# GeGLU feed-forward on one core: the first loads reordered and split by halves of D, the first products regrouped

## The chip, the core and the metric

The kernel runs on one core of a Trainium2 chip. The metric is the device time of one execution in microseconds (us), taken as the median of repeated runs. Beside the timed runs there is one execution that was profiled; all rows below come from it.

## What is computed

```python
B, S, D, F = 32, 32, 1024, 3584        # bf16: x [B, S, D], w_gate and w_up [D, F], w_down [F, D]

def reference(x, w_gate, w_up, w_down):
    return (_gelu(x @ w_gate) * (x @ w_up)) @ w_down      # _gelu: the tanh form
```

There are 1024 tokens (B times S). F is cut into 28 blocks of 128 columns, D into 8 slices of 128.

## The kernel before

**Stage 1** forms `gT`, the gated activations with F on the partitions. It does not multiply the gate and the up product separately. For one block `i` of 128 columns of F it treats the pair (gate, up) and the pair (first 512 tokens, second 512 tokens), with D cut into two halves, as one 2 by 2 block product, and computes it with seven half-size products instead of eight (Strassen's scheme in Winograd's form). A product is four matmuls, one for each 128-row slice of a half of D, each with 512 tokens moving.

The names of the seven products follow the code. The tokens' side: `xt0` holds the first 512 tokens transposed, with halves of D `B11` and `B21`; `xt1` holds the second 512 with `B12` and `B22`. VectorE (DVE) makes from them `T1 = B12 - B11`, `T2 = B22 - T1`, `T3 = B22 - B12`, `T4 = B21 - T2` (line 157, ten instructions, in this order) and ScalarE (ACT) copies `B22`. The weights' side: `a11`, `a12` are the two halves of D of a block of w_gate, `a21`, `a22` those of w_up. For each block the sums `S1 = a21 + a22` (line 166), `S3 = a11 - a21` (line 167), `S2 = S1 - a11` (line 171) and `S4 = a12 - S2` (line 175) are made. `early_sums` makes S1 and S3, `second_sum` S2, `late_sums` S4. S2 is always made by DVE; the others by DVE for the first blocks, and by GpSimd (POOL) later.

- `first_product` (P1) and `second_product` (P2) are the gate of the first tokens: they need only `xt0` and w_gate, and both end in PSUM tile `a`. ACT copies `a` after P1 to SBUF (tile `e1`, line 187) and applies the gelu after P2 (line 193).
- `seed` puts the copy back into another PSUM tile, `X`, on which P6 (S2 with T2), P7 (S3 with T3) and P4 (C22, a copy of a22, with T4) add up in turn. Between them ACT copies `X` out: `E2` after P6 (line 214) and `e3` after P7 (line 227). P4 may only start on `X` when the copy `e3` is done.
- P5 (S1 with T1) and P3 (S4 with B22) add up in PSUM tile `Y`. DVE adds `Y` and `e3` to `U1` (line 229) before P3, and `Y` and `E2` to `h1` (line 234) after it; ACT applies the gelu to `h1` (line 236); `finish` (line 239) multiplies.

PSUM has eight banks here: four for `X` (tag p) and four that `A` and `Y` use in turn (tag q).

Nothing is scheduled by a planner: the order of each engine's instructions is the order in which the code is written (`tc.manual_schedule()`), and tiles add the waits. At the start, 18 matmuls on a zeroed tile (line 137) run while the first loads are under way. All loads go through the queue of SyncE (SP) in program order, except the first half of w_gate tile 0, which ACT issues after the fourth of those matmuls. A w_gate tile (`load_gate`, line 84) holds two blocks of F, 0.52 MB; `load_up(0, 0, 2)` (line 91) brings w_up for blocks 0 and 1, also 0.52 MB; each transposing load of 512 tokens is 1.05 MB.

Since T1 to T4 need the second tokens, the kernel first does P1 of blocks 0 to 7 and P2 of blocks 0 to 6 ("ahead", `LEAD = 8`): 60 matmuls. Then come P5 of blocks 0 and 1 (line 271), P1 of 8 and P2 of 7, P6 of 0 and of 1, P7 of 0 and of 1, P1 of 9 and P2 of 8, P4 of both, P3 of both. The loop over the blocks 2 to 27 follows; it keeps P1 and P2 two blocks ahead through `ahead()`. In it POOL's tiles S1, S3 and S4 have two buffers each, so block `i` reuses those of block `i - 2`.

After `T4`, POOL copies eight elements of it to a tile `held` (line 252). The copy's value is not used: it makes POOL wait until DVE has made T4.

**Stage 2** multiplies `gT` by w_down with the same seven-product scheme (lines 328 to 485) and stores the result.

Of the kernel before, what the change touches and what calls it, by code (L numbers as in the profile page):

```python
# [7 lines left out]
ACT = mybir.ActivationFunctionType  # L8
# [4 lines left out]
def kernel(  # L13
# [35 lines left out]
    assert N == 2 * NB and DT % 2 == 0 and D % DB == 0 and FT % 4 == 0  # L49
    NWARM = 18  # L50
    LEAD = 8
# [29 lines left out]
    def load_gate(c, queue, lo=0, hi=DT):  # L81
        if c not in WG:
            WG[c] = gw.tile([P, DT, 2 * P], bf16, name="gw", tag="gw")
        queue.dma_start(
            out=WG[c][:, lo:hi, :], in_=wg_r[:, lo:hi, 2 * c * P : (2 * c + 2) * P]
        )
# [41 lines left out]
    with tc.manual_schedule():  # L128
# [5 lines left out]

        nc.sync.dma_start_transpose(out=xt0, in_=xf[0:NB, :])
        for n in range(NWARM):
            nc.tensor.matmul(warm[n % 4], lhsT=zt[:, 0:P], rhs=zt, start=True, stop=True)
            if n == 3:
                nc.scalar.activation(table, warm[n][:, 0:8], ACT.Copy)
                load_gate(0, nc.scalar, 0, KH)  # L140
        load_gate(0, nc.sync, KH, DT)
        load_gate(1, nc.sync)
        load_up(0, 0, 2)
        load_gate(2, nc.sync)
        load_gate(3, nc.sync)
        nc.sync.dma_start_transpose(out=xt1, in_=xf[NB:N, :])
        load_gate(4, nc.sync)
# [33 lines left out]

        def first_product(i):
            A[i] = psum_q("a")
            product(A[i], a11(i), B11)
            if i % 2 == 0:
                E1[i // 2] = ring.tile([P, 2, NB], fp32, name="e1", tag="ring")
            nc.scalar.activation(E1[i // 2][:, i % 2, :], A[i], ACT.Copy)  # L187

        def second_product(i):
            product(A[i], a12(i), B21, first=False)  # L190
            if i % 2 == 0:
                GL[i // 2] = half.tile([P, 2, NB], bf16, name="gl0", tag="half")
            nc.scalar.activation(GL[i // 2][:, i % 2, :], A[i], ACT.Gelu_apprx_tanh)

# [5 lines left out]

        done = 0

        def ahead():
            nonlocal done
            if done < FT:
                first_product(done)
            if done:
                second_product(done - 1)
            done += 1

        def sixth_product(i):
            product(X[i], S2[i], T["T2"], first=False)
            E2[i] = epool.tile([P, NB], fp32, name="e2", tag="e2")
            nc.scalar.activation(E2[i], X[i], ACT.Copy)  # L214

# [7 lines left out]

        def seventh_product(i):
            product(X[i], S3[i], T["T3"], first=False)
            e3 = epool.tile([P, NB], fp32, name="e3", tag="e3")
            nc.scalar.activation(e3, X[i], ACT.Copy)  # L227
            U1[i] = epool.tile([P, NB], bf16, name="u1", tag="u1")
            nc.vector.tensor_tensor(U1[i], Y[i], e3, ALU.add)  # L229

# [17 lines left out]
        t_sum("T4", B21, T["T2"])  # L248
        early_sums(2, nc.vector)
        second_sum(2)  # L250
        held = spool.tile([P, 8], f32r, name="held", tag="held", bufs=1)
        nc.gpsimd.tensor_copy(held, T["T4"][:, KH - 1, 0:8])

        between = {2: lambda: copy_a22(0), 4: lambda: seed(0), 6: lambda: seed(1)}
        for n in range(0, LEAD, 2):
            first_product(n)
            first_product(n + 1)
            if n in between:
                between[n]()
            second_product(n)  # L260
            if n + 2 < LEAD:
                second_product(n + 1)
        done = LEAD
        for k in range(KH):
            nc.scalar.activation(T["B22"][:, k, :], B22[:, k, :], ACT.Copy)
        copy_a22(1)
        for i in range(2):
            Y[i] = psum_q("y")
        for k in range(KH):
            for i in range(2):  # L270
                nc.tensor.matmul(  # L271
                    Y[i],
                    lhsT=S1[i][:, k, :],
                    rhs=T["T1"][:, k, :],
                    start=(k == 0),
                    stop=(k == KH - 1),
                    skip_group_check=True,
                )
        ahead()
        sixth_product(0)  # L280
        sixth_product(1)
        seventh_product(0)
        seventh_product(1)
        ahead()
        seed(2)
        fourth_product(0)
        fourth_product(1)
        third_product(0)
        third_product(1)
        late_sums(2)  # L290
        copy_a22(2)
        finish(0)
# [3 lines left out]
        for i in range(2, FT + 1):  # L296
            here, prev, more = i < FT, i - 1 if i > 2 else None, i + 1 < FT
            if more:
                early_sums(i + 1)
            if here:  # L300
                sixth_product(i)
                if more:
                    seed(i + 1)
# [11 lines left out]
            if here:  # L315
                seventh_product(i)
                if more:
                    copy_a22(i + 1)
# [197 lines left out]
```

## Time and profile before

| | |
|---|---|
| median of 3 runs | 277.79 us (277.77 to 277.86) |
| the profiled execution's own time | 277.56 us |
| its span, first to last instruction | 275.8 us |
| TensorE (PE) busy | 270.0 us, 98% |
| DVE, ACT, POOL busy | 189.2, 138.1, 88.6 us |
| first real product starts | 7.96 us after the span's start |
| PE's share of the chain that ended last | 96% |

In the rows, a line such as `7.96 6.85 PE a L113 x31` gives the start in the span, the length, the engine, the tile written, the source line and the count. `T<-xt,xt` reads "tile T from xt and xt". What stands in brackets is the idle time before the row and what ended it. SPq and ACTq are the instruction queues that issue DMAs; the length of such a row is the time of issuing, not of the transfer.

### The profile page before, as it was taken

How to read it: one execution, taken by the hardware profiler on the slowest of the kernel's cores; microseconds unless marked ns; L12 is line 12 of the kernel's file. 1: busy time of each engine (PE TensorE's matmuls, PEld its weight loads, DVE VectorE, ACT ScalarE, POOL GpSimd, SP SyncE). 2: the span in 40 equal slices, each digit the busy share in tenths (PEclk: the TensorE clock that was granted, in tenths of full speed). 3: DMA queues.
4: the chain of work that ended last, by engine and by line, in shares of the span. 5: the costliest groups of instructions: out<-in, count | busy, mean ns of one | idle time of the engine just before them, and what ended most of it. 6: DMA issues, size and time to landing. Idle time of an engine off the chain costs nothing.

```text
span 275.8 us, 3328 instructions
## 1 busy us (share of the span) xinstructions
PE 270.0 (98%) x1179; PEld 190.5 (69%) x1194; DVE 189.2 (69%) x227; ACT 138.1 (50%) x237; POOL 88.6 (32%) x81
## 2 busy tenths in 40 slices
PE   8999999999999999999999999999999999999995
PEld 3446767777677776777766777764447888888883
DVE  0279865667666676666766555759994999999900
ACT  2488475665656665666656666532100082870311
POOL 0000484458554585545854444600000000000000
PEclk9999999999999999999999999999999999999999
DMA  8996420522062071152420120259702000000221
GB/s 194 286 280 157 150 71 5 156 77 76 18 212 76 0 225 37 46 154 76 154 76 9 67 58 22 88 188 324 239 0 76 2 0 0 0 2 0 96 96 38
DMA packets 40912, 26.42 MB, mean 96 GB/s; under 512 B 9152, under 2 KB 40896, under 8 KB 40896
## 3 DMA queue, kind: packets, MB, share of 16 engines
q1 hardware_dynamic: 40224, 25.82, 32.0%
q10 hardware_dynamic: 672, 0.39, 0.5%
q8 instruction: 9, 0.15, 0.2%
q14 instruction: 7, 0.06, 0.1%
HBM read 22.02 MB, written 2.10 MB: 87 GB/s over the span
## 4 chain that ended last, share of the span: by engine, by line
PE 96%; DMA 3%; issue 0%; ACT 0%
PE x L113 28%; PE x L371 18%; PE y L113 18%; PE a L113 17%; PE y L371 9%; PE z L371 4%; DMA xt<-in_x_dram 3%; PE y L271 1%; ACT o_sb L483 0%
## 5 line engine op out<-in xcount | busy, mean ns | idle before, releaser
L113 PE MATMUL x<-T,s 128*128 128x512 f32 x224 | 63.5, 408 | 0.0
L113 PE MATMUL a<-xt,gw 128*128 128x512 bf16 x212 | 51.0, 380 | 1.1 <-DMA xt<-in_x_dram 0.4
L175 POOL TENSOR_TENSOR s<-gw,s 128x512 fp32r<-128x512 bf16 x26 | 30.4, 1171 | 62.4 <-PE y L113 61.7
L113 PEld LDWEIGHTS x<-T,s 128*128 128x128 f32 x224 | 41.7, 188 | 10.8 <-ACT e L214 0.4
L229 DVE TENSOR_TENSOR u<-y,e 128x512 bf16<-128x512 f32 x28 | 19.2, 690 | 34.8 <-ACT e L227 34.1
L171 DVE TENSOR_TENSOR s<-s,gw 128x512 fp32r<-128x512 f32 x28 | 40.8, 1457 | 0.0
L113 PEld LDWEIGHTS <-gw 128*128 128x128 bf16 x224 | 20.2, 98 | 27.6 <-issue 5.7
L218 DVE TENSOR_TENSOR gT<-gl,x 128x512 bf16<-128x512 bf16 x28 | 19.1, 686 | 18.4 <-PE x L113 18.4
L236 ACT ACTIVATE gl<-h 128x512 bf16<-128x512 bf16 x28 | 17.7, 631 | 27.4 <-DVE h L234 27.4
L113 PE MATMUL x<-T,c 128*128 128x512 f32 x112 | 30.2, 393 | 0.0
L113 PE MATMUL y<-B,s 128*128 128x512 f32 x112 | 30.0, 391 | 0.0
L167 POOL TENSOR_TENSOR s<-gw,uw 128x512 fp32r<-128x512 bf16 x25 | 29.2, 1168 | 0.0
L166 POOL TENSOR_TENSOR s<-uw 128x512 fp32r<-128x512 bf16 x25 | 29.1, 1164 | 0.0
L187 ACT ACTIVATE e<-a 128x512 f32<-128x512 f32 x28 | 16.7, 597 | 22.9 <-PE a L113 22.8
L113 PE MATMUL y<-T,s 128*128 128x512 f32 x104 | 27.8, 389 | 0.0
L371 PE MATMUL x<-tc,sc 128*128 128x512 f32 x112 | 25.7, 389 | 0.0
L113 PEld LDWEIGHTS y<-B,s 128*128 128x128 f32 x112 | 21.0, 188 | 4.8
L113 PEld LDWEIGHTS x<-T,c 128*128 128x128 f32 x112 | 20.9, 188 | 4.8 <-ACT e L227 0.5
L371 PEld LDWEIGHTS x<-tc,sc 128*128 128x128 f32 x112 | 21.0, 188 | 4.4
L227 ACT ACTIVATE e<-x 128x512 f32<-128x512 f32 x28 | 16.8, 599 | 14.4 <-PE x L113 14.4
L113 PEld LDWEIGHTS y<-T,s 128*128 128x128 f32 x104 | 19.5, 188 | 4.1
L371 PEld LDWEIGHTS <-gT 128*128 128x128 bf16 x112 | 10.9, 98 | 13.2 <-issue 0.3
(52 smaller groups left out, 325.0 us busy)
## 6 DMA issues: line engine op xcount, KB each, us to landing
gw<-in_w_gate_dram SPq DMA_DIRECT2D x13, 512.0 KB, 3.9
uw<-in_w_up_dram SPq DMA_DIRECT2D x6, 1024.0 KB, 6.4
v<-in_w_down_dram SPq DMA_DIRECT2D x5, 512.0 KB, 3.8
v<-in_w_down_dram SPq DMA_DIRECT2D x4, 640.0 KB, 7.9
v<-in_w_down_dram SPq DMA_DIRECT2D x8, 256.0 KB, 4.3
out_dram<-o_sb SPq DMA_DIRECT2D x15, 128.0 KB, 1.7
uw<-in_w_up_dram SPq DMA_DIRECT2D x2, 512.0 KB, 6.0
gw<-in_w_gate_dram ACTq DMA_DIRECT2D x1, 256.0 KB, 4.4
```

Source lines behind the costliest of these rows:

```text
L113: nc.tensor.matmul(ps, lhsT=lhs[:, k, :], rhs=rhs[:, k, :], start=(first and k == 0), stop=(k == KH - 1), skip_group_check=True,)
L166: engine.tensor_tensor(S1[i], a21(i), a22(i), ALU.add)
L167: engine.tensor_tensor(S3[i], a11(i), a21(i), ALU.subtract)
L171: nc.vector.tensor_tensor(S2[i], S1[i], a11(i), ALU.subtract)
L175: engine.tensor_tensor(S4[i], a12(i), S2[i], ALU.subtract)
L187: nc.scalar.activation(E1[i // 2][:, i % 2, :], A[i], ACT.Copy)
L218: nc.vector.tensor_tensor(gT[:, i, 0:NB], GL[i // 2][:, i % 2, :], X[i], ALU.mult)
L227: nc.scalar.activation(e3, X[i], ACT.Copy)
L229: nc.vector.tensor_tensor(U1[i], Y[i], e3, ALU.add)
L236: nc.scalar.activation(G1[i], h1, ACT.Gelu_apprx_tanh)
L271: nc.tensor.matmul(Y[i], lhsT=S1[i][:, k, :], rhs=T["T1"][:, k, :], start=(k == 0), stop=(k == KH - 1), skip_group_check=True,)
L371: nc.tensor.matmul(ps, lhsT=lhs[:, i, t * P : (t + 1) * P], rhs=rhs[:, i, :], start=(first and j == 0 and i == 0), stop=(last and j == JF ...
```

## The change

- Loads: SP first issues the first halves of D of w_gate tiles 0 and 1, then `xt0` as two transposing loads, one for each half of D, then the second halves of w_gate tiles 0 and 1, w_gate tile 2, w_up for blocks 0 and 1, w_gate tile 3, and the second tokens. ACT issues none of them. The bytes ahead of the second tokens are the same as before; w_up for blocks 0 and 1 stands behind w_gate tile 2 where it stood ahead of it.
- 14 zeroed matmuls instead of 18; ACT's small copy from one of them is left out.
- Ahead: P1 of blocks 0 to 3, then P2 of 0 and 1 side by side by pairs of slices, P2 of 2 and 3; then, for blocks 4, 5 and 6, 7, P1 of both and P2 of both. That is 64 matmuls: P2 of block 7 has moved in front of P5.
- Then P5 of 0 and 1, P1 of 8, P6 of 0 and 1 side by side (two slices of one, two of the other), P1 of 9, P7 of 0 and 1 side by side, P2 of 8, and P4, P3 of block 0 followed by P4, P3 of block 1.
- ACT's seeds for blocks 0 and 1 stand after the fourth copy of P1; its copies of a22 stand later by one pair of blocks.
- DVE makes S1, S3 and S2 of block 2 after the two `U1` of blocks 0 and 1, where it made them before. `held` therefore follows T4 directly.
- POOL makes S1 and S3 of block 3 right after `held`, and S4 of block 2 after them; before, it made S4 of block 2 first.
- From block 3 on the loop is the same.

```diff
-    NWARM = 18
+    NWARM = 14
...
-        nc.sync.dma_start_transpose(out=xt0, in_=xf[0:NB, :])
+        load_gate(0, nc.sync, 0, KH)
+        load_gate(1, nc.sync, 0, KH)
+        nc.sync.dma_start_transpose(out=B11, in_=xf[0:NB, 0 : KH * P])
+        nc.sync.dma_start_transpose(out=B21, in_=xf[0:NB, KH * P : D])
+        load_gate(0, nc.sync, KH, DT)
+        load_gate(1, nc.sync, KH, DT)
+        load_gate(2, nc.sync)
+        load_up(0, 0, 2)
+        load_gate(3, nc.sync)
+        nc.sync.dma_start_transpose(out=xt1, in_=xf[NB:N, :])
         for n in range(NWARM):
             nc.tensor.matmul(warm[n % 4], lhsT=zt[:, 0:P], rhs=zt, start=True, stop=True)
-            if n == 3:
-                nc.scalar.activation(table, warm[n][:, 0:8], ACT.Copy)
-                load_gate(0, nc.scalar, 0, KH)
-        load_gate(0, nc.sync, KH, DT)
-        load_gate(1, nc.sync)
-        load_up(0, 0, 2)
-        load_gate(2, nc.sync)
-        load_gate(3, nc.sync)
-        nc.sync.dma_start_transpose(out=xt1, in_=xf[NB:N, :])
         load_gate(4, nc.sync)
         load_up(0, 2, 4)
...
+        def pair_product(ps, lhs, rhs, first, cuts):
+            for lo, hi in zip(cuts, cuts[1:]):
+                for p, l in zip(ps, lhs):
+                    for k in range(lo, hi):
+                        nc.tensor.matmul(
+                            p, lhsT=l[:, k, :], rhs=rhs[:, k, :],
+                            start=(first and k == 0), stop=(k == KH - 1),
+                            skip_group_check=True,
+                        )
...
-        early_sums(2, nc.vector)
-        second_sum(2)
         held = spool.tile([P, 8], f32r, name="held", tag="held", bufs=1)
         nc.gpsimd.tensor_copy(held, T["T4"][:, KH - 1, 0:8])
...
+        split = range(0, KH + 1, 2)
+        for i in range(4):
+            first_products(i)
+        seed(0)
+        seed(1)
+        second_products(0, 1, cuts=split)
+        second_products(2, 3)
+        for i in range(4, LEAD, 2):
+            first_products(i)
+            first_products(i + 1)
+            copy_a22((i - 4) // 2)
+            second_products(i)
+            second_products(i + 1)
...
+        first_products(8)
+        sixth_products(0, 1)
+        first_products(9)
+        seventh_products(0, 1)
+        second_products(8)
+        early_sums(2, nc.vector)
+        second_sum(2)
+        seed(2)
+        early_sums(3)
+        late_sums(2)
         for i in range(2):
...
+            fourth_product(i)
+            third_product(i)
         copy_a22(2)
         finish(0)
...
-            if more:
+            if more and i > 2:
                 early_sums(i + 1)
```

## The prediction

> **What bounds the kernel now.** I read the page first: its busy shares and its chain.
>
> ```profile
> PE 270.0 (98%) x1179; PEld 190.5 (69%) x1194; DVE 189.2 (69%) x227; ACT 138.1 (50%) x237; POOL 88.6 (32%) x81
> PE 96%; DMA 3%; issue 0%; ACT 0%
> ```
>
> TensorE is the bound for the whole span; the rest of the chain is one DMA. The chain in order of time says which.
>
> ```profile
> 0.73 7.18 DMA xt<-in_x_dram
> 7.96 6.85 PE a L113 x31
> 14.86 6.21 PE a L113 x28
> 21.07 1.85 PE y L271 x8
> ```
>
> From 7.96 us to the end PE follows PE, and its waits add up to under 1 us. The change removes no real matmul. So it can only gain before 7.96 us, and it keeps the gain only if everything that PE needs later comes earlier too. The timeline shows who feeds the start (all engines, first 20 us):
>
> ```profile
> 7.96 12.25 PE L113 MATMUL a<-xt,gw 128*128 128x512 bf16 x55 [0.43 <-DMA xt<-in_x_dram]
> 10.13 6.97 SPq L146 DMA_TRANSPOSE xt<-in_x_dram  x1
> 12.25 0.69 DVE L166 TENSOR_TENSOR s<-uw 128x512 fp32r<-128x512 bf16 x1 [11.12 <-DMA uw<-in_w_up_dram]
> 19.26 1.29 DVE L157 TENSOR_TENSOR T<-xt,xt 128x512 fp32r<-128x512 bf16 x2 [1.86 <-DMA xt<-in_x_dram]
> ```
>
> PE waits for the first tokens (issued at 0.73, landed 7.2 us later, 7.9), DVE at 19.26 for the second ones (issued 10.13, landed 9.0 later, 19.1). In between the DMA engines are full, as the windows show (PE, PEld, DVE, ACT, POOL, PEclk, DMA share, GB/s):
>
> ```profile
> 3.75:5.75 2.00, 2.00 (x6) 0.72 (x5) 0.00 (x0) 0.00 (x0) 0.00 (x0) 1.00 1.27 289
> 8.50:18.50 10.00, 9.95 (x47) 4.51 (x46) 5.08 (x8) 7.38 (x13) 0.00 (x0) 1.00 1.22 289
> 40.50:41.00 0.50, 0.50 (x3) 0.24 (x3) 0.50 (x2) 0.00 (x0) 0.19 (x1) 1.00 1.13 339
> ```
>
> Transposed x alone and the mixed loads both move at 289 GB/s, a lone w_gate tile at up to 339. Last, the windows in which the lead is spent (VectorE and GpSimd, then ACT and PE):
>
> ```profile
> 28.49 0.68 DVE L166 TENSOR_TENSOR s<-uw 128x512 fp32r<-128x512 bf16 x1
> 28.63 1.79 POOL L252 CAST held<-T 128x8 fp32r<-128x8 f32 x1 [28.20 <-DVE T L157]
> 34.32 0.69 DVE L234 TENSOR_TENSOR h<-y,e 128x512 bf16<-128x512 f32 x1 [0.70 <-ACT gl L236]
> 35.23 1.35 POOL L167 TENSOR_TENSOR s<-gw,uw 128x512 fp32r<-128x512 bf16 x1
> 35.49 1.64 DVE L171 TENSOR_TENSOR s<-s,gw 128x512 fp32r<-128x512 f32 x1
> 35.05 0.63 ACT L236 ACTIVATE gl<-h 128x512 bf16<-128x512 bf16 x1 [0.76 <-DVE h L234]
> 38.32 0.60 ACT L227 ACTIVATE e<-x 128x512 f32<-128x512 f32 x1
> 39.04 1.13 PE L113 MATMUL x<-T,c 128*128 128x512 f32 x4
> ```
>
> From h1 of block 1 (ends 35.02) ACT runs without a break to the e3 copy of block 2 (ends 38.92), and P4 of block 2 starts at 39.04, 4.02 us after that h1. PE itself would be there at 39.0 too. So there is a second bound with no slack: second tokens, T1 to T4, DVE's queue, ACT's queue, P4 of block 2. After it ACT is idle for 1.58 us at 42, so nothing later is as tight.
>
> **The first tokens.** The two w_gate halves that now go first are 0.52 MB. A copy issued at 38.48 moves nothing until 39.5, so the first byte comes near 0.73 + 1.05 = 1.8. The 0.52 MB take 1.6 (339 GB/s) to 1.8 us (289), plus some 0.4 of ramp (116 and 283 GB/s in its first two half microseconds): done at 3.9. B11, 0.52 MB at 289, is done at 5.7. A landing trails the traffic by 0.6 us (that tile: traffic to 41.6, landed 42.2) to 0.9 (first tokens: traffic to 6.1, then 0.26 MB of the other queue, landed 7.9). So B11 lands at 6.3 to 6.6, I take 6.45. The other end: the same first byte as before and only 0.26 MB less in front of it, 7.9 - 0.9 = 7.0.
>
> **The zeroed matmuls.** The last three of 18 start 6.71 to 7.14, 0.216 apart; with four fewer the next matmul can start at 6.5. PE starts at the later of the two: 6.5 (bound above: 7.05), against 7.96. **Gain at the start 1.45 us** (0.9).
>
> **Does the lead run through?** P1 of four blocks, 16 matmuls of 0.217 (1.74 for 8), lasts to 9.95. B21 lands 1.8 after B11, 8.25; second half of w_gate 0 at 9.15 (needed 9.95), of tile 1 at 10.05 (11.7), tile 2 at 11.85 (13.4), tile 3, behind w_up, at 15.4 (16.9). The tightest has 0.8 us. ACT's two moved seeds (0.60 each) put gelu 0 at 12.4; the bank is needed at 13.4. Dropping ACT's small copy (0.18) and its DMA issue touches nothing: ACT idles there. P5 then starts at 6.5 + 64 x 0.217 = 20.4.
>
> **The second tokens.** The bytes ahead of them are the same, so they land earlier only by the earlier first byte: 1.8 against 2.2, less the ramp, plus faster copies at the start. I take 0.35 (0 to 0.7): 18.8. w_up for blocks 0 and 1 lands one tile (0.52 MB, 1.8 us) later in the order: 12.25 + 1.8 - 0.35 = 13.7; DVE's eight sums took 12.25 to 17.40, so they end at 18.85, just as xt1 arrives. No loss, but no slack either. T1 starts at 18.9, and T4 ends 0.35 earlier, at 28.2 (28.57 before). PE needs the last piece of T1 at 21.8 (ready 21.4), the second half of T2 at 24.0 (23.7), of T3 at 26.7 (25.95), of T4 at 28.9 (28.2). No wait. P6 and P7 side by side cost at most 0.06: the side-by-side P5 took 1.85 for 8 against 1.81.
>
> **DVE after T4, the term that decides.** Before: S1, S3, S2 of block 2, two U1, two gT, two h1; h1 of block 1 ended 6.45 us after T4, with waits of 0.17 for P3 and 0.70 for ACT's gelu. Now: two U1 (e3 of block 1 is ready at 28.3), S1, S3, S2, then gT, h1, gT, h1. Each step is 0.60 after the last. POOL now starts S1 of block 3 some 0.25 after T4 (`held` short, like the 0.10 us POOL memsets; its 1.79 above is a wait) and holds up DVE's S1, issued 1.12 after T4: the last rows show a DVE sum of two SBUF tiles that took 1.64 instead of 0.68, ending 0.54 after POOL's. So DVE's S1 ends at 0.25 + 1.17 + 0.55 = 1.97 after T4, S2 at 3.17, the first h1 at 4.38, gelu at 5.05, the second h1 at 5.77. That is 28.2 + 5.8 = 34.0; P4 of block 2 at 38.0 instead of 39.04. PE alone would have come to 6.5 + 31.1 = 37.6. S2 of block 2, ready at 31.4, is needed by P6 at 32.0. **The later counts: gain 1.05 us.** If `held` did take 1.8, POOL would come after two of the three sums: 0.2 better, or one op's wait (0.9) worse. From block 3 the loop is the same, and loads, POOL and stage 2 move along.
>
> Sum: 277.56 - 1.05 = 276.5 for the profiled execution; the median lies 0.23 above that execution, so 276.75.
>
> **Rivals.** (1) POOL gets in between DVE's sums. After T4 DVE would do S1, wait for POOL's S3 of block 3 (0.9), do S3 and S2. h1 ends at 34.9, P4 of block 2 starts at 38.9, gain 0.15: 277.65. For it: at 35.23 POOL's sum went ahead of DVE's L171 (35.49). Against it: `held` asked at 28.63 and ended at 30.43, only when DVE's three sums in a row (the last 29.69 to 30.38) were through. The Trainium skill ("SBUF — State Buffer", SBUF: two separate sides) says that the port pair shared by the two is locked by whichever op starts first, for that whole instruction, and the other blocks; read strictly, the lock is free after each DVE sum, and 277.65 would come out. The L171 row agrees with the blocking, the `held` row speaks against the strict reading. 15%.
>
> (2) Slower: half-row transposes are slower. Each token's row is now read as two pieces of 1 KB. If that costs rate, B11, B21 and all behind them come late. The bound chain breaks even at T4 ending at 28.57 + (6.45 - 5.8) = 29.2, 1 us later than in my sum: 1.05 MB in 4.6 us instead of 3.6, or 225 GB/s; at 150 GB/s (the lowest full-queue row, 7.25 to 7.50, has 152) T4 ends at 31.6, and the time is 280.2. Against it: x alone moved at the same 289 GB/s as the mixed loads, so the transpose was not what set the rate. The Trainium skill ("DMA: Bandwidth & Descriptors", Latency and other measured facts) gives 261 GB/s for transposes whose middle dimension is not contiguous; by it x comes 0.4 us later and the time is 277.1. No run here shows a half-row transpose yet. 12%.
>
> (3) It doesn't do what it says: both transposes share the DMA engines and land together at 7.9. Then PE starts as before, and the same matmuls end at 277.8. 5%; but w_gate tiles 2 and 3, behind one another in the queue (issued 6.37 and 8.35), landed one by one, at 14.0 and 15.8.
>
> **Numbers.** 0.2%, 0.56 us, is about what a measurement of this kernel can tell from no change. My forecast has 68%, all of it faster. Rival 1 gives "same" with 12 of its 15, the rest slower; rival 3 is same; rival 2 slower. So faster 0.68, same 0.17, slower 0.15. The range goes down to a start bound by the zeroed matmuls alone (1.45, 276.3) and up over rival 1 (277.7).
>
> **What would show it.** In the profile after: the first P1 near 6.5 with little idle time before it; DVE's first T1 near 18.9; `held` short, at 28.3; DVE's S1 of block 2 stretched to some 0.85 and S3, S2 at 0.68; P4 of block 2 near 38.0. Wrong if T1 starts after 19.3, if S3 or S2 is stretched over 1.5, or if PE waits again before block 4.

## The result, and the profile after

The changed kernel takes 279.75 us (median of 6 runs, 279.29 to 280.34), the kernel before 277.78 beside it (277.69 to 277.92). The ratio is 1.0071, with a 95% interval of 1.0058 to 1.0084: slower by 1.97 us, where a gain of 1 us was forecast. The runs also spread over 1.05 us, against 0.23 before. The profiled execution took 279.45 us; its span is 277.7.

First the page of the kernel after (busy shares, then shares of the chain that ended last):

```profile
PE 271.0 (98%) x1190; PEld 189.5 (68%) x1190; DVE 189.1 (68%) x227; ACT 137.8 (50%) x236; POOL 87.4 (31%) x81
PE 86%; DVE 5%; SPq 4%; DMA 3%; issue 1%; ACT 1%; ACTq 0%
```

TensorE is as busy as it was, but its share of the chain fell from 96 to 86%. The chain in order of time (start, length, engine, what) says what took its place:

```profile
...
10.20 1.74 SPq L84
11.98 8.74 DMA xt<-in_x_dram
20.74 2.57 DVE T L157 x5
...
30.05 1.20 DVE u L248 x2
...
32.07 1.57 DVE s L167
...
34.38 1.16 PE x L186 x4
...
40.66 1.18 PE x L113 x4
```

Up to P4 of block 2 (40.66) the end is set by SyncE's queue, the second tokens' transpose, T1 to T4, VectorE's sums, and some steps of TensorE and ACT between them. The prediction had this chain as a second bound with no slack; now it is the first. The timeline of all engines shows the starts of TensorE and of T1:

```profile
7.34 14.14 PE L186 MATMUL a<-xt,gw 128*128 128x512 bf16 x64 [1.29 <-DMA xt<-in_x_dram]
15.55 0.69 DVE L166 TENSOR_TENSOR s<-uw 128x512 fp32r<-128x512 bf16 x1 [14.42 <-DMA uw<-in_w_up_dram]
20.74 1.90 DVE L157 TENSOR_TENSOR T<-xt,xt 128x512 fp32r<-128x512 bf16 x3
```

TensorE starts at 7.34 after 1.29 us idle: 0.62 earlier than before, not 1.45. The 64 matmuls then run nearly through. But T1 starts at 20.74, where before it started at 19.26. Two things come together there. The second tokens land at 20.72. And w_up for blocks 0 and 1 lands only at 15.53 (12.23 before), so that VectorE's eight sums are done only at 20.71 (the last takes 0.69 from 20.02). Second tokens that came earlier would alone have won about 0.1 us. Both are loads. The windows of the start (PE, PEld, DVE, ACT, POOL, PEclk, DMA share, GB/s) show why:

```profile
4.50:5.50 1.00, 1.00 (x6) 0.45 (x5) 0.00 (x0) 0.00 (x0) 0.00 (x0) 1.00 1.25 130
5.50:6.50 1.00, 0.55 (x3) 0.15 (x2) 0.00 (x0) 0.00 (x0) 0.00 (x0) 1.00 1.27 284
8.50:9.75 1.25, 1.25 (x8) 0.54 (x7) 0.00 (x0) 0.98 (x2) 0.00 (x0) 1.00 0.55 140
10.00:16.00 6.00, 6.00 (x29) 2.57 (x28) 0.45 (x1) 4.93 (x9) 0.00 (x0) 1.00 1.14 301
16.25:17.00 0.75, 0.75 (x6) 0.29 (x4) 0.75 (x2) 0.67 (x2) 0.00 (x0) 1.00 1.21 141
```

Between three holes the traffic moves at 284 to 301 GB/s, the half-row transposes too (5.50 to 6.50). The holes lie where the first transpose follows the two copies (130 GB/s for 1 us), behind the transposes (140 for 1.25 us) and where the second tokens' transpose begins (141 for 0.75 us). Measured against 289 GB/s they lose 0.55, 0.64 and 0.38 us, 1.57 in all; the second tokens landed at 20.72 instead of 19.17, 1.55 later. The match is rough: the kernel before has a dip of its own (152 GB/s from 7.25 to 7.50), and the first bytes now move earlier. The holes are of two kinds. Behind the transposes the DMA engines' share is low (0.55); where a transpose begins among copies, the share stays high (1.25 and 1.21) while little moves.

VectorE's and GpSimd's rows after T4:

```profile
31.17 0.90 DVE L166 TENSOR_TENSOR s<-uw 128x512 fp32r<-128x512 bf16 x1
31.99 1.64 DVE L167 TENSOR_TENSOR s<-gw,uw 128x512 fp32r<-128x512 bf16 x1
33.56 0.68 DVE L171 TENSOR_TENSOR s<-s,gw 128x512 fp32r<-128x512 f32 x1
```

```profile
30.12 0.19 POOL L269 CAST held<-T 128x8 fp32r<-128x8 f32 x1 [29.67 <-DVE T L157]
30.35 1.17 POOL L166 TENSOR_TENSOR s<-uw 128x512 fp32r<-128x512 bf16 x1
31.48 1.61 POOL L167 TENSOR_TENSOR s<-gw,uw 128x512 fp32r<-128x512 bf16 x1
```

`held` is short. DVE's S1 waits for POOL's S1, then POOL's S3 comes in between and DVE's S3 is stretched to 1.64. PE's rows for block 2 follow:

```profile
34.38 1.16 PE L186 MATMUL x<-T,s 128*128 128x512 f32 x4 [0.37 <-DVE s L171]
38.55 2.11 PE L186 MATMUL x<-T,s 128*128 128x512 f32 x8 [0.33 <-ACT e L231]
40.65 1.19 PE L113 MATMUL x<-T,c 128*128 128x512 f32 x4
```

P4 of block 2 starts 1.61 later than before (40.65 against 39.04): T4 1.48 later (30.05 against 28.57), 0.33 more from T4 to the end of h1 of block 1 (6.78 against 6.45), 0.20 less from there to P4 (3.82 against 4.02). The execution is 1.89 longer.

### The profile page after: what moved, and what is told of

Its sections match the earlier page's. It is cut to its first block, busy times and chain, and to the rows that moved or that the text cites. A ratio compares the mean times of both kernels' runs of the same rounds, so it can differ in the third digit from the quotient of the medians.

```text
span 277.7 us, 3338 instructions
## 1 busy us (share of the span) xinstructions
PE 271.0 (98%) x1190; PEld 189.5 (68%) x1190; DVE 189.1 (68%) x227; ACT 137.8 (50%) x236; POOL 87.4 (31%) x81
## 4 chain that ended last, share of the span: by engine, by line
PE 86%; DVE 5%; SPq 4%; DMA 3%; issue 1%; ACT 1%; ACTq 0%
PE x L384 18%; PE x L186 17%; PE y L113 17%; PE a L186 11%; PE y L384 9%; PE x L113 9%; PE z L384 4%; DMA xt<-in_x_dram 3%; DVE T L157 3%; SPq L84 2%; SPq L137 1%; SPq L138 1%; DVE s L167 1%; SPq L91 1%; DVE u L248 0%
## 5 line engine op out<-in xcount | busy, mean ns | idle before, releaser
L186 PE MATMUL a<-xt,gw 128*128 128x512 bf16 x224 | 52.5, 380 | 1.3 <-DMA xt<-in_x_dram 1.3
L248 DVE TENSOR_TENSOR u<-y,e 128x512 bf16<-128x512 f32 x28 | 19.3, 691 | 35.8 <-ACT e L246 35.2
L171 DVE TENSOR_TENSOR s<-s,gw 128x512 fp32r<-128x512 f32 x28 | 39.9, 1424 | 0.0
```

What stands on the lines that cost most here:

```text
L171: nc.vector.tensor_tensor(S2[i], S1[i], a11(i), ALU.subtract)
L186: nc.tensor.matmul(p, lhsT=l[:, k, :], rhs=rhs[:, k, :], start=(first and k == 0), stop=(k == KH - 1), skip_group_check=True,)
```

## The experiments

Three theories stand in the expectations, which were written before each run. **Split:** a transpose of half rows is slow in itself, so x and all behind it come late. **Queue, or cover:** what costs is the order in the queues. A copy ahead of a transpose in its queue makes a hole; and SyncE issues a transpose for so long that the copy behind it comes late, unless another queue has one ready, as ACT's queue had before. **P:** POOL's two sums ahead of S4 get in between DVE's sums. Each theory's price is worked out in the expectations.

All results are here, ahead of the single runs. The median and ratio (with its interval) are against runs of the kernel before on the same chip; the other columns are from the profiled execution: start of the first product, landing of the second tokens, end of T4, time from there to the end of h1 of block 1, start of P4 of block 2, and the execution's own time.

| kernel | median | ratio | first P1 | second tokens | T4 | T4 to h1 | P4 (2) | own time |
|---|---|---|---|---|---|---|---|---|
| before | 277.78 | | 7.96 | 19.17 | 28.57 | 6.45 | 39.04 | 277.56 |
| after | 279.75 | 1.0071 (1.0058 to 1.0084) | 7.34 | 20.72 | 30.05 | 6.78 | 40.65 | 279.45 |
| e1 | 278.53 | 1.0029 (1.0017 to 1.0040) | 7.93 | 19.19 | 28.59 | 7.36 | 39.85 | 278.43 |
| e2 | 280.32 | 1.0092 (1.0075 to 1.0109) | 9.23 | 21.07 | 30.40 | 7.68 | 41.97 | 280.63 |
| e3 | 279.13 | 1.0052 (1.0034 to 1.0071) | 8.14 | 21.84 | 31.18 | 5.59 | 40.59 | 279.42 |
| e4 | 279.47 | 1.0057 (1.0042 to 1.0072) | 7.04 | 20.07 | 29.41 | 6.78 | 40.01 | 278.83 |
| e5 | 281.51 | 1.0128 (1.0102 to 1.0154) | 10.12 | 21.49 | 30.83 | 8.04 | 42.88 | 281.52 |
| e6 | 282.70 | 1.0180 (1.0161 to 1.0199) | 10.44 | 21.24 | 30.57 | 9.55 | 44.02 | 282.72 |
| e7 | 278.02 | 1.0010 (1.0001 to 1.0018) | 6.25 | 20.48 | 29.81 | 5.59 | 39.22 | 278.00 |
| e8 | 277.87 | 1.0009 (1.0000 to 1.0018) | 7.98 | 19.27 | 28.67 | 6.75 | 39.24 | 277.85 |
| f1 | 278.43 | 1.0032 (1.0020 to 1.0044) | 8.45 | 20.18 | 29.51 | 6.19 | 39.62 | 278.30 |
| f2 | 278.06 | 1.0014 (1.0005 to 1.0024) | 8.13 | 20.02 | 29.42 | 6.19 | 39.51 | 278.09 |
| f3 | 278.14 | 1.0020 (1.0010 to 1.0029) | 8.05 | 20.11 | 29.51 | 5.67 | 39.61 | 278.19 |
| f4 | 278.07 | 1.0020 (1.0007 to 1.0033) | 6.50 | 20.09 | 29.42 | 5.59 | 38.83 | 277.64 |
| g1 | 277.24 | 0.9985 (0.9976 to 0.9994) | 6.35 | 19.74 | 29.07 | 5.59 | 38.48 | 277.28 |
| g2 | 279.40 | 1.0071 (1.0047 to 1.0094) | 10.75 | 21.03 | 30.43 | 8.71 | 43.16 | 281.72 |
| g3 | 277.67 | 1.0001 (0.9992 to 1.0010) | 8.09 | 19.38 | 28.78 | 5.93 | 39.14 | 277.74 |

In all 17 executions the own time is P4 of block 2 plus 238.5 to 238.8 us. Whatever a kernel does at the start, its time is decided there. The columns from the profile are one execution each, and kernels with holes spread: f4's rows are from an execution 0.43 us below its median, e4's from the fastest of its four, g2's from the slowest of its seven.

**e1, the changed work with the loads of before.**

```diff
-        load_gate(0, nc.sync, 0, KH)
-        load_gate(1, nc.sync, 0, KH)
-        nc.sync.dma_start_transpose(out=B11, ...)
-        nc.sync.dma_start_transpose(out=B21, ...)
+        # the load block of before, 18 zeroed matmuls
```

> The order of products, sums and seeds of the changed kernel, with the loads and the 18 zeroed matmuls of the kernel before. Separates the loads from the order of work. Theory L (the loads cost the time: the second tokens land 1.55 us later) and theory P (GpSimd's sum gets in between VectorE's three sums, and h1 of block 1 ends 6.8 us after T4 instead of 6.45) both leave the start as it was before: first P1 at 7.96, T1 at 19.3, T4 ends at 28.6. Under L alone P4 of block 2 starts no later than 39.0 and the time is 277.8 or less. Under P as well, h1 of block 1 ends at 35.35, P4 of block 2 starts at 39.2, and the time is 277.9 to 278.1, so that the loads carry 1.6 to 1.9 of the 1.97 us.

The second tokens land at 19.19 and T4 ends at 28.59, as before: the T4 term of the loss is due to the loads. The rest isn't clean: with P1 of block 2 third in line, PE now waits 0.69 us at 10.51 for w_gate tile 1, which here still comes as a whole, and P4 of block 2 starts at 39.85 where 39.2 was expected. So the ratio falls only from 1.0071 to 1.0029: about 1.2 us of the loss goes with the loads, not the expected 1.6 to 1.9.

**e2, x in one transpose behind the two copies.**

```diff
-        nc.sync.dma_start_transpose(out=B11, ...)
-        nc.sync.dma_start_transpose(out=B21, ...)
+        nc.sync.dma_start_transpose(out=xt0, in_=xf[0:NB, :])
```

> The changed kernel with the first tokens transposed by one load instead of two, still behind the two first halves of w_gate. Theory split (half-row transposes are issued and moved slower: 2.70 + 2.42 us of issue against 3.80 before): the issue takes 3.8 again, the second tokens land at 19.2 to 19.4 instead of 20.7, P4 of block 2 starts near 39.5, time 278.5 or less, although PE's first P1 waits for all of the first tokens (near 8.2). Theory queue (the transposes' issue holds SyncE's queue while the DMA engines have nothing behind it, whatever the cut): the traffic has the same hole of about 1 us after the transposes, the second tokens land at 20.2 to 20.7, first P1 near 8.5, time 279.3 to 280.

Without the split it is no better: x lands at 9.19, as late as the second half in the kernel after. The windows show the hole in front again, 141 GB/s from 4.00 to 5.75. The split is not what makes it. The second tokens (21.07) and the median come out worse than either theory said; the clock, told at the end, has a part in the median.

**e3, POOL's S4 of block 2 ahead of its S1 and S3 of block 3.**

```diff
-        early_sums(3)
-        late_sums(2)
+        late_sums(2)
+        early_sums(3)
```

> The changed kernel with GpSimd's S4 of block 2 ahead of its S1 and S3 of block 3, as before the change; loads untouched. S4 of block 2 needs VectorE's S2, so GpSimd cannot touch VectorE's three sums. Theory P: VectorE's S1, S3, S2 of block 2 take 0.68 each, h1 of block 1 ends 5.6 to 5.7 us after T4 instead of 6.8, P4 of block 2 starts near 39.6 instead of 40.65, time 278.6 to 278.8. Rival (VectorE's sums are not what P4 of block 2 waits for; the loads alone set it): within 0.2 us of the changed kernel, 279.6.

A row of VectorE's timeline after T4:

```profile
32.89 0.69 DVE L167 TENSOR_TENSOR s<-gw,uw 128x512 fp32r<-128x512 bf16 x1
```

S1 and S3 are back at 0.69, and T4 to h1 is 5.59 instead of 6.78: POOL's place cost 1.19 us of this stretch. In this execution the loads, unchanged, landed 1.1 later than in the kernel after (21.84), which hides it in the single time. So the landing behind the holes varies from run to run, which fits the wide spread of both kernels (1.05 and 1.62 us). The medians, 279.13 and 279.75, have overlapping intervals of the ratio.

**e4, both front halves issued by ACT at the start.**

```diff
-        load_gate(0, nc.sync, 0, KH)
-        load_gate(1, nc.sync, 0, KH)
+        load_gate(0, nc.scalar, 0, KH)
+        load_gate(1, nc.scalar, 0, KH)
         nc.scalar.activation(table, ...)
```

> The changed kernel with the first halves of w_gate tiles 0 and 1 issued by ScalarE's queue at the very start, so that SyncE begins with the two half-row transposes at 0.73. Theory queue: both transposes are issued by 4.6, the loads behind them stand in the queue in time, the traffic has no hole; the second tokens land at 18.8 to 19.2, T4 ends at 28.2 to 28.6, h1 of block 1 ends 6.8 later by theory P, P4 of block 2 at 39.0 to 39.4, time 277.6 to 278.0. Theory split: issue still takes 2.7 + 2.4 us, the second tokens land after 19.7, time 278.7 or more. A third possibility: the two queues share the DMA engines so that the transposes go first and the w_gate halves land only after them, near 7.5 to 8; then PE starts no earlier than before.

The holes shrink but stay: 180 GB/s from 5.75 to 6.75, 144 from 8.00 to 9.25. The second tokens come 0.65 earlier than in the kernel after, in the fastest of the four executions; the medians, 279.47 and 279.75, have overlapping runs. Theory queue had asked for no hole and 278.0 at most, so as written it missed; the numbers lie where theory split put them (after 19.7, 278.7 or more).

**e5, the split alone, in the kernel before.**

```diff
-        nc.sync.dma_start_transpose(out=xt0, in_=xf[0:NB, :])
+        nc.sync.dma_start_transpose(out=B11, in_=xf[0:NB, 0 : KH * P])
+        nc.sync.dma_start_transpose(out=B21, in_=xf[0:NB, KH * P : D])
```

> The kernel before, with one edit: the first tokens are loaded by two half-row transposes instead of one, still first in SyncE's queue, nothing in front of them. Theory split (half-row transposes are slower by themselves): their issue takes 4.5 us or more together instead of 3.80, the second half lands at 8.5 or later, the second tokens at 19.7 or later, time 278.3 or more. Theory queue (it is the copies in front of the transposes, and the lack of copies behind them, that make holes in the traffic): issue 3.8 to 4.0 together, second half at 7.9, second tokens at 19.2, time 277.6 to 277.8, as before, since the first product also waits for w_gate, which lands at 7.6.

As written, theory queue is refuted here and theory split is met (278.3 or more), but 281.51 is far above what either had a price for, and the two issues take 4.1 us together, not the 4.5 or more of split. The first half lands at 5.32, the second only at 10.36, w_gate 0's first half at 10.07. A window of e5:

```profile
4.50:9.00 4.50, 2.03 (x10) 0.71 (x8) 0.00 (x0) 0.00 (x0) 0.00 (x0) 1.00 1.20 182
```

The DMA engines are busy (share 1.20), yet only 182 GB/s move for 4.5 us, where 267 moved from 3.00 to 4.50. It begins near the boundary between the two transposes, with ACT's copy, issued near 3.2, still to come. Either the split or that meeting does it; f1 takes the meeting away.

**e6, the second halves on ACT's queue as cover, issued early.**

```diff
+            if n == 3:
+                nc.scalar.activation(table, warm[n][:, 0:8], ACT.Copy)
+                load_gate(0, nc.scalar, KH, DT)
+                load_gate(1, nc.scalar, KH, DT)
...
-        load_gate(0, nc.sync, KH, DT)
-        load_gate(1, nc.sync, KH, DT)
```

> The changed kernel, with the second halves of w_gate tiles 0 and 1 issued by ScalarE's queue after the fourth zeroed matmul (where the kernel before issued its first load) instead of by SyncE behind the transposes. The copies in front of the transposes stay. Theory queue, hole behind: the traffic after the second transpose (8.5 to 9.75 us, 13 to 51 KB in a quarter us against 72) is filled, the second tokens land 0.7 to 1.0 earlier than 20.72, P4 of block 2 as much earlier, time 278.8 to 279.1. If the hole in front (4.5 to 5.5 us) is all that counts: less than 0.3 better, 279.5 or more.

It was to help, and it is the slowest of all: 143 GB/s from 6.00 to 8.00, with the engines' share at 1.27, and x only at 10.40 and 11.81. Here the copies of the second queue that came in between the transposes did worse than none.

**e7, one front half on ACT's queue, cover, POOL later.**

```diff
         # at the start
+        load_gate(0, nc.scalar, 0, KH)
         # after the fourth zeroed matmul
+        load_gate(1, nc.scalar, 0, KH)
+        load_gate(0, nc.scalar, KH, DT)
         # SyncE: B11, B21, second half of tile 1, the rest; sums as in e3
```

> All three causes taken away at once. ScalarE issues the first half of w_gate tile 0 at the very start, and after the fourth zeroed matmul the first half of tile 1 and the second half of tile 0; SyncE begins with the two half-row transposes at 0.73 and goes on with the rest; GpSimd makes S4 of block 2 ahead of its sums of block 3. If copies in front of the transposes, no copies ready behind them, and GpSimd between VectorE's sums are the whole loss, then: B11 lands at 6.0 to 7.0, first P1 at 6.5 to 7.1, second tokens at 18.8 to 19.4, h1 of block 1 ends 5.6 us after T4, P4 of block 2 starts at 38.0 to 38.5, time 276.7 to 277.3, which beats both kernels. Theory split, or a cost of the regrouped products that is not yet seen: 277.8 or more.

x's first half lands at 6.21 and PE starts at 6.25, near the forecast start, but the second tokens still land at 20.48: 278.02, with 1.7 us of the loss gone, and not the 276.7 to 277.3 that the three causes together were to give. ACT's two copies came in between the transposes here too (landed at 7.24 and 8.18, the second half at 9.79), yet 276 GB/s moved from 4.00 to 9.00: they delayed the second half and made no hole like those of e5 and e6.

**e8, the new order of the sums alone, in the kernel before.**

```diff
-        early_sums(2, nc.vector)
-        second_sum(2)
         held = ...
...
+        early_sums(2, nc.vector)
+        second_sum(2)
+        seed(2)
+        early_sums(3)
+        late_sums(2)
```

> The kernel before with its own loads and products, except the order of sums after T4, which is that of the changed kernel: VectorE makes S1, S3, S2 of block 2 after the two U1, GpSimd makes S1 and S3 of block 3 right after held and S4 of block 2 after them, and P4, P3 go block by block. Theory P: VectorE's S1 takes 0.9 and S3 1.6 us, h1 of block 1 ends 6.8 to 6.9 after T4 (35.4) instead of 6.45, P4 of block 2 starts at 39.3 to 39.5, time 278.0 to 278.2. Rival (the collision costs nothing because PE has other work): 277.8, no difference.

The edit also runs P4 and P3 block by block, as the changed kernel does.

VectorE's and GpSimd's timelines:

```profile
30.59 1.65 DVE L167 TENSOR_TENSOR s<-gw,uw 128x512 fp32r<-128x512 bf16 x1
```

```profile
30.08 1.61 POOL L167 TENSOR_TENSOR s<-gw,uw 128x512 fp32r<-128x512 bf16 x1
```

The same stretched S3 as after, with landings as before. P is a real mechanism, but its price to the kernel is 0.2 us here (277.87 against 277.67; the interval touches no change), less than expected: with these loads h1 comes only 0.3 later than in the kernel before.

**f1, the split, with one queue.** As e5, with w_gate 0's first half on SyncE's queue behind x.

```diff
-                load_gate(0, nc.scalar, 0, KH)
...
+        load_gate(0, nc.sync, 0, KH)
         load_gate(0, nc.sync, KH, DT)
```

> The kernel before with the first tokens as two half-row transposes first in SyncE's queue, and with the first half of w_gate tile 0 issued by SyncE right behind them; ScalarE issues no load. Differs from the run with the split alone (281.51, second half landed at 10.36) only in the queue of that one w_gate load. Theory mix (a transpose that stands behind another one loses its rate when copies of another queue come in between): with one queue the traffic is steady, both halves are issued by 4.6, the second lands at 7.0 to 7.5, the second tokens at 19.2 to 19.8, time 277.8 to 278.3. Theory split (two half-row transposes are slower, whatever stands beside them): the second half lands at 8.5 or later and the second tokens after 20, time 279 or more.

**f2, the same on the kernel before, x whole.** The diff is that of f1.

> The kernel before with one edit: the first half of w_gate tile 0 is issued by SyncE right behind the first tokens, not by ScalarE. One transposing load first, nothing in front of it and no second queue. It prices the cover: SyncE can issue the next load only at 4.6, so the traffic should have a dip of about half a us after the transpose ends at 6.1. Theory cover: dip of 0.4 to 0.7 us, second tokens at 19.5 to 19.9, T4 0.3 to 0.7 later than 28.57, P4 of block 2 0.3 to 0.7 later, time 278.1 to 278.5. If a load ready in a second queue is not needed: second tokens at 19.2, time 277.7 to 277.9.

f1's second half lands at 7.12, as theory mix had it, though its second tokens are at 20.18 (f2's at 20.02). With one queue the split costs the second tokens 0.16 us and the median 0.37; e5 had lost 2.3 and 3.8 against the kernel before. So the split in itself is not what makes the loss, and that theory falls as the main cause. And f2 prices the copy that stood ready in ACT's queue: without it the second tokens are 0.85 late and the kernel 0.4 us slower, close to what theory cover had said. Two windows of f2 (behind the first transpose, and where the second tokens' transpose begins), then the same two places in the kernel before:

```profile
6.00:7.00 1.00, 1.00 (x6) 0.34 (x4) 0.00 (x0) 0.00 (x0) 0.00 (x0) 1.00 0.84 190
15.50:16.50 1.00, 1.00 (x6) 0.47 (x5) 1.00 (x3) 0.73 (x2) 0.00 (x0) 1.00 1.24 161
```

```profile
6.00:7.00 1.00, 1.00 (x7) 0.47 (x5) 0.00 (x0) 0.00 (x0) 0.00 (x0) 1.00 1.19 320
14.75:15.75 1.00, 0.95 (x6) 0.42 (x5) 1.00 (x3) 0.78 (x2) 0.00 (x0) 1.00 1.25 282
```

Behind the first transpose 320 GB/s move with the second queue's copy and 190 without it, at a lower share of the engines. That is not the whole price. Where the second tokens' transpose begins, f2 has a second hole (161 GB/s, worth 0.44 us against 289), which the kernel before has not (282), with the same loads right ahead of it in the queue. What makes this one isn't shown. The cover has a price of its own: in f2 x lands at 6.78, in the kernel before at 7.91; f2 gains nothing by it because w_gate's half lands at 8.08.

**f3, the kernel before with ACT's load at the very start,** 14 zeroed matmuls and the sums of g3.

```diff
+        load_gate(0, nc.scalar, 0, KH)     # ahead of the table activation
-                load_gate(0, nc.scalar, 0, KH)
```

> Candidate for a version that beats both. Loads of the kernel before, but ScalarE issues its w_gate load at the very start instead of after the fourth zeroed matmul; 14 zeroed matmuls; VectorE's and GpSimd's sums in the order that needs 5.6 us from T4 to h1 of block 1 (GpSimd's S4 of block 2 first). x stays one transposing load, first in SyncE's queue. If one copy ready before the transpose starts does no harm: it lands near 4, x at 6.9 to 7.3, first P1 at 7.0 to 7.4, second tokens at 19.2 to 19.6, P4 of block 2 at 38.2 to 38.6, time 277.0 to 277.4. If a copy in front of a transpose makes a hole, as in the changed kernel: x at 7.8 or later, second tokens at 20 or later, time 278 or more.

The same 0.26 MB, moved from cover to front, costs the second tokens 0.94 us, about as in f2, though x lands hardly later than before (8.01). The median, 278.14, is where the second alternative put it: no version that beats both.

**f4, e7 without ACT's two later copies.**

```diff
-                load_gate(1, nc.scalar, 0, KH)
-                load_gate(0, nc.scalar, KH, DT)
...
+        load_gate(1, nc.sync, 0, KH)
+        load_gate(0, nc.sync, KH, DT)
```

> The run with all three causes taken away (278.02), without ScalarE's two later copies: ScalarE issues only the first half of w_gate tile 0, at the very start; all else stands in SyncE's queue behind the two half-row transposes. It tells whether those two copies, which went ahead of the second transpose and held SyncE's issue until 7.83, are what kept that run from 277. Theory mix: second half lands at 8.0 to 8.6 instead of 9.79, second tokens at 19.5 to 20.0 instead of 20.48, P4 of block 2 at 38.3 to 38.9, time 277.1 to 277.7. Theory split: second tokens at 20.3 or later, 278 or more.

x lands at 5.89 and 7.76 instead of 6.21 and 9.79: those two copies, issued near 3.2, had got between the transposes. But PE waits 1.03 us at 9.42 for tile 1, and the runs spread from 277.41 to 279.09. The median, 278.07, is no better than e7's 278.02, so taking those two copies out won nothing by itself.

**g1, f4 with ACT's copies later,** after the eighth zeroed matmul.

```diff
-        load_gate(1, nc.sync, 0, KH)
-        load_gate(0, nc.sync, KH, DT)
...
+            if n == 7:
+                nc.scalar.activation(table, warm[n % 4][:, 0:8], ACT.Copy)
+                load_gate(1, nc.scalar, 0, KH)
+                load_gate(0, nc.scalar, KH, DT)
```

> The run with one front load on ScalarE's queue (278.07; second tokens at 20.09, traffic dip from 7.0 to 8.0 behind the second transpose), with the first half of w_gate tile 1 and the second half of tile 0 issued by ScalarE after the eighth zeroed matmul (4.8 us, when the first transpose is nearly through), not by SyncE at 5.75. If a load that stands ready in the second queue fills the dip without getting between the transposes: second tokens at 19.5 to 19.7, T4 ends at 29.0, h1 of block 1 5.6 later, P4 of block 2 at 38.3 to 38.5, time 277.0 to 277.3, better than both kernels. If it gets between the transposes or among the second one's packets, as the copies issued at 3.19 did: second half lands after 9, second tokens at 20.2 or later, time 278 or more.

A window of g1, and PE's timeline:

```profile
7.00:8.00 1.00, 1.00 (x6) 0.39 (x4) 0.00 (x0) 0.58 (x1) 0.00 (x0) 1.00 1.19 316
```

```profile
6.35 1.89 PE L188 MATMUL a<-xt,gw 128*128 128x512 bf16 x8
38.48 1.19 PE L113 MATMUL x<-T,c 128*128 128x512 f32 x4
```

No hole behind the transposes: 316 GB/s from 7.00 to 8.00, where f4 has 174. PE starts at 6.35 and waits once, 0.74 us for tile 1; P4 of block 2 starts at 38.48, 0.56 earlier than before. The landing (19.74), T4 (29.07) and the time come out about as expected. The median is 277.24 against 277.64, the ratio 0.9985 (0.9976 to 0.9994): the version that beats both kernels, by 0.4 us over the one before.

**g2, a copy in front with the cover kept,** in the kernel before: w_gate 0's first half on SyncE's queue ahead of the whole x, its second half on ACT's queue in place of the first.

```diff
+        load_gate(0, nc.sync, 0, KH)
         nc.sync.dma_start_transpose(out=xt0, in_=xf[0:NB, :])
...
-                load_gate(0, nc.scalar, 0, KH)
-        load_gate(0, nc.sync, KH, DT)
+                load_gate(0, nc.scalar, KH, DT)
```

> The kernel before with the first half of w_gate tile 0 moved in front of the first tokens in SyncE's own queue, and the second half of the tile put in its place in ScalarE's queue, so that the cover behind the transpose stays and x is one load. It prices a copy in front of a transpose alone. If the front copy costs what the changed kernel lacks beyond the cover (20.72 against 20.02): second tokens at 19.6 to 20.0, time 277.9 to 278.3. If the lost cover is the whole cost: second tokens at 19.2 or earlier, since the traffic starts earlier, and time 277.6 to 277.8.

The window of g2:

```profile
4.50:5.50 1.00, 1.00 (x4) 0.38 (x3) 0.00 (x0) 0.00 (x0) 0.00 (x0) 1.00 1.58 62
```

One copy ahead of one whole transpose is enough for the hole in front, 62 GB/s for 1 us, and SyncE then takes 5.80 us to issue the transpose (3.80 in the kernel before). The second tokens are 1.9 late and the median is 1.8 us worse, both more than expected. The profiled execution is the slowest of its seven (281.72; the others lie from 278.56 to 279.67), so its rows tell the place of the hole rather than its usual price.

**g3, e8 with POOL's S4 first,** as in e3.

```diff
-        early_sums(3)
         late_sums(2)
+        early_sums(3)
```

> The kernel before with its own loads and products, and the sums after T4 in the order that kept GpSimd out of VectorE's way: VectorE makes S1, S3, S2 of block 2 after the two U1, GpSimd S4 of block 2 ahead of its sums of block 3, P4 and P3 block by block. h1 of block 1 should end 5.6 to 5.8 after T4 (34.3) instead of 6.45, 0.7 ahead of the kernel before; PE has no start to gain, so P4 of block 2 stays at 38.9 to 39.1 and the time at 277.5 to 277.8. Against the run with GpSimd first (277.87) that is 0.2 less. If the order of P4 and P3 by block costs something: 277.9 or more.

277.67 against 277.64. With POOL later the sums cost nothing; DVE's are 0.68, 0.68 and 0.69. h1 waits 0.29 us for PE now, so the order gains nothing on its own either.

## Why the prediction was wrong

**What held.** The bound chain: second tokens, T1 to T4, DVE, ACT, P4 of block 2. The prediction's sum from its own form, with the measured T4 and rival 1's step (34.9 - 28.2 = 6.7), is 30.05 + 6.7 + 4.02 = 40.8, and 40.65 was measured. The lead runs through but for one stall of 0.15 at 10.94, where the second half of w_gate 0 landed at 10.90 and not at 9.15. The eight sums and the arrival of xt1 tie, as said, only 1.9 us later: the last sum is done at 20.71, T1 starts at 20.74. All three of its own signs of being wrong are there: T1 after 19.3, an S3 stretched over 1.5 and, with that stall of 0.15, PE waiting again before block 4. P4 of block 2 misses 38.0 by 2.65: 1.85 by T4 and 0.98 by DVE after T4, less 0.20 in ACT's part. The zeroed matmuls were not in the way. The copies in front were done at about 4.1, not far from 3.9.

**The step that failed, first: "The bytes ahead of them are the same, so they land earlier only by the earlier first byte".** Bytes at a rate were taken for the landing, 18.8, with 19.17 as the worst. It was 20.72. Equal bytes moved in holes and full stretches, and changing nothing but the order and queue of the loads brings the holes and takes them away (e1, f2, g1). The same step had w_up at 13.7; it landed at 15.53. e1 shows the part of the loads as a whole. f2 shows what it costs to take out a copy that ACT's queue had ready: 0.85 us of landing, of which the hole where the second tokens' transpose begins is about half ("Dropping ACT's small copy (0.18) and its DMA issue touches nothing" had costed it at nothing). g2, with the cover kept, shows the hole in front. The single prices don't add up (0.85, and 1.86 in g2's slowest execution, against 1.55 together), so each is only that of its own kernel. The same step missed B11 by the hole at 4.5 to 5.5: 7.30, outside 6.3 to 7.0, so the gain at the start was 0.62, not 1.45.

**The step that rests on it: "The later counts: gain 1.05 us".** The rule held; its terms did not. T4 came 1.85 us later than forecast, so the 0.62 at the start was worth nothing. TensorE needs 27.04 us from its first product to P6 of block 2 (25.68 before; 116 matmuls in both), with P5 of blocks 0 and 1 at 2.54 instead of 2.20 and 0.37 of idle time for DVE's S2, and from there 6.27 to P4 of block 2 (5.40 before), with 0.33 of idle time for ACT's copy. g1 is the counter-test: T4 at 29.07, only 0.5 later than before, 5.59 from T4 to h1, and a gain at the end.

**The second step that failed: DVE after T4, forecast 5.8, was 6.78.** That is rival 1, as written there (its gelu and P4 followed as described): the stretched op is S3, by POOL's S3. The row that was to speak against it, `held` at 1.79, is no rule. With the order of before, where DVE's three sums follow T4, `held` took 1.79 in f1 and f2 too, but 0.59 in e5 and g2; in e5 it was through at 31.48, when of the three sums only the first was done (S3 from 31.35, S2 from 31.96). What decides between the two isn't shown. The Trainium skill ("SBUF — State Buffer", SBUF: two separate sides) has the pair locked for one instruction. The traces of the kernel after and e8, where the two engines take turns, agree; in the kernel before, f1 and f2 GpSimd did not get in between VectorE's sums. With POOL's order as in e3 the forecast 5.8 is nearly met, 5.59.

**Rival 2** gave the sign and the break-even (T4 at 29.2, passed by 0.85), but by luck, not by its mechanism: half rows move at 284 GB/s here, whole rows at 289, and f1 against f2 costs 0.16 us. The Trainium skill ("DMA: Bandwidth & Descriptors", Latency and other measured facts) has 261 GB/s for its non-contiguous case, below both rows. **Rival 3** did not happen: the halves landed at 7.30 and 9.19.

**Open.** What happens inside the DMA engines in a hole isn't shown; only the traffic, the share and the issue times are. Nor is it shown when a transpose behind copies begins with a hole: the kernel after, e2 and g2 have one at the first transpose, the kernel after and f2 at the second tokens' transpose, the kernel before none there. Nor why ACT's copies do harm issued near 3.2 in e5 and e6, but made no such hole in e7, and none issued at 4.9 in g1. The 0.12 us lost between P4 of block 2 and stage 2 (1.61 against 1.73) was not followed.

## What to carry to other kernels

A load's landing time is not the bytes ahead of it over a rate: look in the windows for what fills the DMA engines while one queue is busy issuing a long transpose, and count a copy that waits ready in a second queue as part of the design. Look there also for holes where a transpose begins behind copies (the kernel after, e2, g2) and where copies come in between two transposes (e5, e6). Neither is a rule here: the second tokens' transpose of the kernel before begins behind copies without one, and e7's copies made none. Before counting a gain at the start, follow every chain that meets it later: here 0.62 us at the front was lost to 1.55 us in a load with the same bytes ahead of it as before.

## What the runs showed of the hardware

- **Issue and traffic.** SyncE's issue of the second tokens' transpose takes 6.7 to 7.2 us with copies in flight; that of the first 3.80 in the kernel before and 3.93 in f2, with nothing in front, but 5.37 in e2 and 5.80 in g2 with copies in front, and 5.17 in f3, where the copy in front is in ACT's queue. With the split, the second half's issue took 5.6 us in e7 and 2.42 in the kernel after.
- **Busy engines, little traffic.** The DMA share stayed at 1.20 to 1.58 while 62 to 182 GB/s moved (e5, e6, g2). The share alone would have hidden the holes; the GB/s column shows them.
- **A cold TensorE.** In e2, e5, e6 and g2, where x came so late that PE was idle for 2.1 to 4.0 us, the granted clock fell to 0.50, and matmuls came 0.427 us apart instead of 0.216. In e6 and g2 it fell before PE went on, in e2 and e5 about half a microsecond to a microsecond after. This is e5 (the seventh column is the clock):

```profile
12.00:14.00 2.00, 2.00 (x6) 0.72 (x5) 0.00 (x0) 0.76 (x2) 0.00 (x0) 0.50 1.20 291
```

This adds to these executions a loss that the loads alone don't explain; in g2 only the profiled execution has it. After idle times of 0.5 to 1.3 us in the kernel after, e4, e7 and g1 there was none. The length of the idle time alone does not decide it: e3 was idle for 2.44 us and kept the full clock, e2 lost it after 2.13.
- **The zeroed matmuls start cold as well.** They come 0.427 us apart at first and 0.216 once the clock is full, which was from 3.8 to 6.7 us after the span's start (5.83 in the kernel before, 4.61 after). So the time when 14 of them are through varies from one execution to the next, and the forecast 6.5 held only for some: in f4 and g1 the first product follows the last zeroed matmul directly, at 6.50 and 6.35.
- **`held`,** a copy of eight elements, took 0.19 us in the twelve executions where DVE had only U1 or nothing to do after T4, and beside DVE's three sums 1.79 (before, f1, f2) or 0.59 (e5, g2).
